# A retention and gated-MLP kernel on one core: w_sg transposed once, u's half of w_in in two loads, a new job order

## The chip, the cores and the metric

The kernel runs on one core of a Trainium2 chip, as one program. The metric is device microseconds of one execution, and the median over several runs is compared. Engines are named as in the profile: PE is TensorE, DVE is VectorE, ACT is ScalarE, POOL is GpSimd, SP is SyncE, which here only issues DMAs.

## The reference

Retention over 8 batches, 8 heads, 576 positions and head size 64, then a gated MLP that mixes along the sequence. All in float32.

```python
scores = scale * q @ k^T                       # per batch and head, 576 x 576
ret = scores * where(i >= j, gamma_h ** (i - j), 0)
x = (ret @ v), heads side by side              # 8 x 576 x 512
h = gelu_tanh(x @ w_in)                        # w_in 512 x 1024
u, v = h[..., :512], h[..., 512:]
v_n = (v - mean(v)) / sqrt(var(v) + 1e-6) * g_ln
v_s = einsum('ts,bsd->btd', w_sg, v_n) + b_sg  # w_sg 576 x 576, along the sequence
out = x + (u * v_s) @ w_out                    # w_out 512 x 512
```

## The kernel before

Two batches make a pair of 1152 rows, nine tiles of 128. Tile 4 (MID) holds the last 64 rows of the first batch and the first 64 of the second. A pair is worked in five blocks (`RB`): blocks 0 and 1 of the first batch and 3 and 4 of the second have two tiles each, block 2 is the middle tile. There are four pairs, so 20 blocks and 36 tiles. Decay is put into q and v as row factors, so that inside a block a mask is enough, and what earlier positions of the batch give comes in through a running sum of k^T v.

For a block, SP loads q, k and v in float32 (`a_load`). POOL scales and casts them to bf16 (`a_prep`; for block 0, DVE does q and ACT does k). PE transposes q and k into PSUM (`a_T`) and DVE copies them to `qT`, `kT` (`a_Tev`); from block 10 on most of this is done by DMA transposes (`a_TX`). q of some blocks is loaded for two blocks at once (blocks 3 and 4, 5 and 6, and so on). Blocks 0, 1 and the middle ones are "joint": q and k share one tile and one transpose. Then PE makes scores (`a_S`), DVE masks them (`a_Sev`), PE makes k^T v (`a_Z`) and the retention output (`a_O`, `a_O2`), and ACT writes it as x, transposed, into `xT` (`a_Oev`).

For a tile, PE makes V's half of the hidden layer (`m_V`), ACT its gelu (`m_Vg`), DVE the statistics (`m_stats`), POOL the inverse root (`m_rs`), ACT the normalised `vn` (`m_norm`). PE makes u's half (`m_U`) and ACT its gelu (`m_Ug`). When a batch's tiles are normalised, PE multiplies by w_sg transposed (`m_W`, eight jobs a batch of five matmuls each), DVE multiplies the result into u (`m_Wg`), PE makes the output product (`m_O`), the residual is added (for the first pair by a PE matmul with the identity, for the others from an SBUF copy made by a DMA transpose, `m_X`), and SP stores it.

A batch's sequence begins at row 0 of a tile for the first batch of a pair and at row 64 of MID for the second, so w_sg transposed is kept twice: `wT[0]` for the first and `wT[1]`, shifted by 64 rows, for the second. w_sg is loaded by rows in float32 into a staging tile, cast by ACT into `wnat` (L413), and ten builds (`build_wT`, L921) of five PE transposes each, one for each 128 columns of each set, give ten PSUM tiles that DVE copies out (`evac_wT`, L925). `wnat` has 64 zero columns on either side, so that the shifted set falls out of the same transposes. Four spare rows of the middle tiles carry b_sg and the inverse of g_ln: `place_vmid` (L909, L910) and `place_wT` (L913, L914) write them from `row4b`, which comes from `to_col`, `col_math`, `to_rows` and `rows`.

The weights w_in (its halves `win_load(1)` for V, `win_load(0)` for u, 1 MB each), w_sg and w_out come through staging tiles that borrow the buffers of `xT` and `uT`. Each half of w_in is cast by DVE (L388) and ACT (L390) together, into the bf16 `w_in`.

Each of these steps is a job. A written-out list, `ORDER`, gives every job by its number; entries with f are filler matmuls of zeros (`fill`, L357). A planner (`Planner.follow`) takes each engine's jobs in the list's order, computes a start for each by estimated durations, and emits all jobs sorted by it. Every engine executes its own jobs strictly in that order, so a job that waits holds back all behind it on its engine. PSUM has two large buffers (tag `pp`: transposes, scores, retention outputs) and four small ones (tag `d`: everything else). SBUF buffers go round by tag: eight for loads of k, v and single q (`ld`), two for double q (`ldq`).

Before the first W job TensorE's queue holds, in this order of first appearance: filler, block 0's transposes and scores, filler, block 0's outputs, block 1, V of tiles 0 and 1, then block 2 and V of tiles 2 to 4 among the ten builds, block 3's transposes, u of blocks 0 to 2, scores and outputs of block 3. SP's queue begins: q, k, v of block 0, V's half of w_in, the last rows of w_sg, q, k, v of block 1, w_sg in two loads, q, k, v of block 2, q of blocks 3 and 4, u's half of w_in, k of 3, k of 4, v of 3, k of 6, v of 4, k of 5, q of blocks 5 and 6, w_out.

Of the kernel before, what the change touches and what calls it, by code (L numbers as in the profile page):

```python
# [17 lines left out]
SEM = {"PE": 205.0, "DVE": 35.0, "ACT": 35.0, "POOL": 35.0}  # L18
OVL = {"PE": 0.0, "DVE": 60.0, "ACT": 90.0, "POOL": 50.0, "SP": 0.0}
FETCH = (5400.0, 5000.0)  # L20
SWITCH = {("F", "Q"): 95.0, ("F", "T"): 95.0, ("Q", "F"): 140.0, ("Q", "T"): 90.0, ("T", "F"): 5.0, ("T", "Q"): 5.0}

# [58 lines left out]
class Planner:  # L81


    def __init__(self, bufs, free, slack=60.0, penalty=500.0, fill=None, fill_until=0.0):
        self.bufs, self.free = bufs, free
        self.slack, self.penalty = slack, penalty
        self.fill, self.fill_until = fill, fill_until
        self.jobs, self.order = [], {t: [] for t in bufs}
        self.dma_free, self.dmas, self.ring = 0.0, [], []
        self.mode, self.warm = None, False  # L90
        self.count, self.block, self.landed = 36, 1, 0.0
        self.port = 0.0
# [6 lines left out]
    def ready(self, j):  # L99
        t = max(self.free[j.eng], j.since)  # L100
        if j.port:
            t = max(t, self.free["POOL"])
        if j.eng == "POOL":
            t = max(t, self.port)
        if j.behind is not None:
            if j.behind.start is None:
                return None
            t = max(t, j.behind.start + 100.0)
        for d in j.deps:
            if d.start is None:  # L110
                return None
            lat = 166.0 if (d.eng == "DVE" and j.eng == "POOL") else SEM.get(d.eng, 0.0)
            if d.eng == j.eng:
                lat = j.lag if j.eng == "PE" else 60.0
            if j.eng == "PE" and d.eng != "PE":
                lat += 20.0
            t = max(t, d.out + lat)
        took = {}
        for b in j.new:
            o, n = self.order[b.tag], self.bufs[b.tag]  # L120
            at = len(o) - n + took.get(b.tag, 0)
# [10 lines left out]
    def place(self, j, t):  # L132
# [31 lines left out]
        if j.port:  # L164
            self.port = j.out
# [1040 lines left out]
```

## Time and profile before

| | |
|---|---|
| median of 3 runs | 213.02 us (211.63 to 214.35) |
| span of the profiled execution, first to last instruction | 211.8 us |
| mean granted TensorE clock | 0.992 |
| busy: PE, DVE, ACT, POOL | 193.5, 146.7, 116.3, 117.9 us |
| moved by DMA | 50.45 MB, mean 238 GB/s |

The profiled execution has no time apart from its span; the three timed runs stand on both sides of it. "Busy" counts time in which at least one instruction of the engine runs. A row of a timeline gives start, duration, engine, line, operation, output and input, and in brackets how long the engine stood idle before it and what ended that. A row of windows gives the stretch and its length, each engine's busy time with the count of instructions, the granted clock, the DMA share and GB/s. A group's row gives busy time and mean nanoseconds after the first bar, idle time and releasers after the second.

### The profile page before, as it was taken

The page shows a single profiled execution, that of the slowest core. Times are in us where ns is not written, and L with a number is a line of the kernel's source. Part 1 is how long each engine was busy: PE and PEld are TensorE (multiplying, and loading weights), DVE is VectorE, ACT ScalarE, POOL GpSimd, SP SyncE. Part 2 cuts the span into 40 slices and gives each one's busy share as a digit, 9 for nine tenths or more (in the row PEclk, how much of TensorE's full clock was granted, in tenths as well). Part 3 has the DMA queues.
Part 4 walks back from the last instruction along what each step waited for, and adds up shares of the span by engine and source line. Part 5 has one row for each costly group of instructions (what it writes and reads, how often), then busy time and mean ns, then how long its engine had stood idle before and what let it go on. Part 6 is the DMA issues. An engine that isn't in the chain of part 4 may idle for free.

```text
span 211.8 us, 7654 instructions
## 1 busy us (share of the span) xinstructions
PE 193.5 (91%) x3257; PEld 134.4 (63%) x3288; DVE 146.7 (69%) x287; ACT 116.3 (55%) x207; POOL 117.9 (56%) x169
## 2 busy tenths in 40 slices
PE   7995598799999999989999979989989999999992
PEld 6873366576677666757676657656647676565660
DVE  4585487978767688648767647778676757977483
ACT  5233656993696753784775745617544574363400
POOL 8738375897599699920849598044349440322000
PEclk9999889999999999999999999999999999999999
DMA  5999899999799999999898989999789986936685
GB/s 157 334 274 323 140 377 273 259 347 320 146 316 319 317 208 289 181 258 326 245 253 110 219 155 345 237 129 248 197 217 264 254 193 187 225 115 149 176 249 198
DMA packets 94228, 50.45 MB, mean 238 GB/s; under 512 B 45354, under 2 KB 87602, under 8 KB 94194
## 3 DMA queue, kind: packets, MB, share of 16 engines
q1 hardware_dynamic: 94176, 49.97, 96.9%
q8 instruction: 25, 0.41, 0.9%
q14 instruction: 9, 0.07, 0.2%
q10 hardware_dynamic: 18, 0.00, 0.0%
HBM read 32.79 MB, written 9.44 MB: 199 GB/s over the span
## 4 chain that ended last, share of the span: by engine, by line
PE 62%; DMA 16%; SPq 5%; POOL 5%; DVE 3%; ACT 3%; issue 3%; POOLq 0%; ACTq 0%
PE wp L807 15%; PE op L838 11%; PE hu L788 11%; PE hv L741 11%; PE pp L673 5%; DMA xT<-in_moe_w_sg_dram 4%; DMA xT<-in_moe_w_in_dram 4%; PE pp L591 3%; DMA ld<-in_k_dram 3%; DMA kT<-kb 3%; SPq L560 3%; DMA ld<-in_q_dram 2%; PE zp L627 2%; SPq L457 2%; POOL vb L503 2%
## 5 line engine op out<-in xcount | busy, mean ns | idle before, releaser
L604 DVE TENSOR_TENSOR ret<-pp,msk 128x1024 bf16<-128x1024 f32 x32 | 38.7, 1216 | 6.4 <-PE pp L591 6.4
L503 POOL TENSOR_TENSOR vb<-ld,gpow 128x1024 bf16<-128x1024 f32 (+1 forms) x20 | 34.6, 1731 | 14.7 <-DMA ld<-in_v_dram 9.1
L807 PE MATMUL wp<-wT,vn 128*128 128x288 bf16 x256 | 40.8, 286 | 0.0
L788 PE MATMUL hu<-xT,w_in 128*128 128x256 bf16 (+1 forms) x320 | 36.7, 262 | 0.2 <-ACT zb L659 0.2
L741 PE MATMUL hv<-w_in,xT 128*128 128x512 bf16 x125 | 35.1, 380 | 1.4 <-issue 0.3
L817 DVE TENSOR_TENSOR uT<-wp,uT 128x288 bf16<-128x288 f32 x64 | 27.9, 449 | 11.5 <-PE wp L807 11.0
L838 PE MATMUL op<-w_out,uT 128*128 128x512 bf16 (+1 forms) x136 | 34.3, 373 | 0.6
L730 ACT ACTIVATE xT<-pp 128x512 bf16<-128x512 f32 (+1 forms) x40 | 20.6, 552 | 25.8 <-PE pp L673 24.0
L788 PEld LDWEIGHTS <-w_in 128*128 128x128 bf16 x320 | 28.2, 98 | 7.0 <-issue 0.5
L756 DVE BATCH_NORM_STATS2 bst<-vg 128x6 f32<-128x512 f32 x36 | 24.7, 687 | 10.1 <-ACT vg L748 10.0
L776 ACT ACTIVATE vn<-vg,mv 128x512 bf16<-128x512 f32 x32 | 25.3, 807 | 11.1 <-POOL mv L764 11.0
L748 ACT ACTIVATE vg<-hv 128x512 f32<-128x512 f32 x36 | 21.3, 594 | 17.0 <-PE hv L741 13.3
L807 PEld LDWEIGHTS <-vn 128*128 128x128 bf16 x256 | 24.2, 98 | 8.4 <-issue 0.2
L761 POOL TENSOR_SCALAR mv<-mv 128x2 f32<-128x2 f32 (+1 forms) x20 | 4.5, 224 | 42.2 <-DVE mv L757 38.3
L503 POOL TENSOR_TENSOR qb<-ldq,gpow 128x1024 bf16<-128x1024 f32 x14 | 26.5, 1902 | 0.9 <-DMA ldq<-in_q_dram 0.8
L798 ACT ACTIVATE uT<-hu 128x512 bf16<-128x512 f32 x36 | 20.9, 595 | 7.9 <-PE hu L788 7.9
L855 DVE TENSOR_TENSOR ob<-op,xr 128x512 f32<-128x512 f32 (+1 forms) x28 | 18.4, 668 | 6.1 <-PE op L838 5.8
L838 PEld LDWEIGHTS <-uT 128*128 128x128 bf16 x148 | 13.7, 98 | 11.5
L741 PEld LDWEIGHTS <-xT 128*128 128x128 bf16 x144 | 13.2, 98 | 11.6 <-ACT xT L730 0.2
L807 PE MATMUL wp<-wT,vmid 128*128 128x288 bf16 x64 | 18.3, 287 | 0.0
L493 POOL CAST kb<-ld 128x1024 bf16<-128x1024 f32 x14 | 14.4, 1038 | 4.3 <-DMA ld<-in_k_dram 4.2
L762 POOL TENSOR_TENSOR mv<-mv,mhalf 128x2 f32<-128x2 f32 (+1 forms) x20 | 13.7, 686 | 1.7
(100 smaller groups left out, 248.9 us busy)
## 6 DMA issues: line engine op xcount, KB each, us to landing
out_dram<-ob SPq DMA_DIRECT2D x35, 256.0 KB, 3.5
ld<-in_k_dram SPq DMA_DIRECT2D x16, 512.0 KB, 6.9
ld<-in_v_dram SPq DMA_DIRECT2D x16, 512.0 KB, 6.7
ldq<-in_q_dram SPq DMA_DIRECT2D x7, 1024.0 KB, 8.4
xT<-in_moe_w_sg_dram SPq DMA_DIRECT2D x2, 576.0 KB, 9.0
ld<-in_q_dram SPq DMA_DIRECT2D x2, 512.0 KB, 6.3
xT<-in_moe_w_in_dram SPq DMA_DIRECT2D x1, 1024.0 KB
ld<-in_q_dram SPq DMA_DIRECT2D x8, 128.0 KB, 5.9
```

The costliest lines, as they stand in the source:

```text
L503: ve.tensor_tensor(dst, src, g.unsqueeze(len(src.shape) - 1).to_broadcast(list(src.shape)), op=Alu.mult)
L604: ins = nc.vector.tensor_tensor(ret[:].rearrange("p r (k t) -> p (r k) t", k=2), sc[:].rearrange("p r (k t) -> p (r k) t", k=2), (msk2 if ...
L730: nc.scalar.activation(dst, src, Act.Copy)
L741: ins = nc.tensor.matmul(hv[:], xTs[p][:, m, kk, :], w_in[:, kk, F2:], start=(kk == 0), stop=(kk == KK - 1))
L748: unfence(nc.scalar.activation(vgs[i][:], cur.pop(("hv", i))[:], Act.Gelu_apprx_tanh), ("V", i))
L756: nc.vector.bn_stats(bst[:], vgs[i][:])
L776: nc.scalar.activation(vn[:], vg[:], Act.Identity, scale=mv[:, s, 2:3], bias=mv[:, s, 3:4])
L788: ins = nc.tensor.matmul(hu[:, n, :], w_in[:, kk, 128 * c:128 * c + 128], xTs[p][:, m:m + w, kk, :], start=(kk == 0), stop=(kk == KK - 1), ...
L798: unfence(nc.scalar.activation(uTs[p][:, c0:c1, 128 * m:128 * m + 128 * w], cur.pop(("hu", i, half))[:], Act.Gelu_apprx_tanh), ("U", i, half))
L807: ins = nc.tensor.matmul(ps[:], vns[t0 + j][e][:, 128 * c:128 * c + 128], wT[e][j][:, half * HS:(half + 1) * HS], start=(j == 0), stop=(j ...
L817: ins = nc.vector.tensor_tensor(uTs[p][:, c, col:col + HS], cur.pop(("wp", b, c, half))[:], uTs[p][:, c, col:col + HS], op=Alu.mult)
L838: ins = nc.tensor.matmul(op[:], uTs[p][:, c, r], w_out[:, c, cs], start=(p >= XP and c == 0), stop=(c == KK - 1), skip_group_check=True)
```

## The change

`wT[0]` and `wT[1]` become one tile each. Five builds, one for each 128 rows of w_sg, transpose into PSUM, and DVE copies each into `wT[0]`; the last holds 64 rows. ACT copies `wT[0]` into `wT[1]` shifted by 64 partitions, in nine copies of 64 x 576 (`shift_wT`). The jobs of batch 0 wait for the five copies and one `place_wT`; those of batch 1 for the nine shifts and the other. The memset of `wT[0]`'s spare rows goes.

u's half of w_in comes in two loads of half the columns, each cast by DVE and ACT. u's first job for a two-tile block waits for the first half, the second job for the second. For block 0 the transposes leave PSUM in two halves, by DVE and ACT.

The planner's estimates are gone: the new `ORDER` is emitted as it stands. Its only fillers are `f1` and the new order is different for every engine. TensorE now begins: one small filler, `to_col`, block 0's transposes, both `to_rows`, block 0's scores and k^T v, block 1's transposes, k^T v of block 1, block 0's outputs, block 1's scores, V of tile 0, and so on; transposes of block 3's q stand ahead of block 2's; u's first job stands after V of tile 2, and four jobs of u for blocks 3 and 4, after k^T v of block 4, stand before the first W job (two of them) and among the first W jobs (two). SP's queue begins: k, q, v of block 0, q, v, k of block 1, V's half of w_in, q of blocks 3 and 4, q and k of block 2, the last rows of w_sg, the first half of u's w_in, v of 2, k of 3, k of 4, the second half of u's w_in, w_sg's first load, v of 3, w_sg's second, v of 4, k of 5, k of 6, q of blocks 5 and 6, w_out. `place_vmid` moves on ACT from behind V's gelu of tile 4 to before that of tile 0. On DVE `col_math` and the two `rows` stand before block 0's mask, and the cast of V's half of w_in before block 1's `a_Tev`.

```diff
     def plan(self):
-        if ORDER:
-            return self.follow(ORDER)
...
+        self.done = [self.fill(int(x[1:])) if x[0] == "f" else self.jobs[int(x)] for x in ORDER.split()]
...
-    wnat = consts.tile([128, SB, S + 128], BF, name="wnat")
+    wnat = consts.tile([128, SB, S + 64], BF, name="wnat")
...
-    wT = [[consts.tile([128, S], BF, name=f"wT{e}_{j}") for j in range(SB)] for e in range(2)]
+    wT = [consts.tile([128, SB, S], BF, name=f"wT{e}") for e in range(2)]
...
+        parts = 1 if half else 2
+        w = F2 // parts
...
+        def g(part, a, eng):
+            src = wst["in", half][:, 2 * a:2 * a + 2, w * part:w * part + w]
...
+    def a_Tev(b, t, c=None):
...
+        if c is None:
+            ins = nc.vector.tensor_copy(dst, src)
+        elif c == 0:
+            ins = nc.vector.tensor_copy(dst[:, 0], src[:, 0])
+        else:
+            ins = nc.scalar.activation(dst[:, 1], src[:, 1], Act.Copy)
...
-    def build_wT(e, j):
-        c0 = (64 if e == 0 else 0) + 128 * j
-        tp = psD.tile([128, SB * 128], BF, name="wtp", tag="d")
...
-    def evac_wT(e, j):
-        r = slice(0, NB0) if (e, j) == (0, SB - 1) else slice(NB0, 128) if (e, j) == (1, 0) else slice(0, 128)
-        nc.vector.tensor_copy(wT[e][j][r, :], cur.pop(("wtp", e, j))[r, :S])
+    def build_wT(t):
+        tp = psD.tile([128, SB, 128], BF, name="wtp", tag="d")
+        cur["wtp", t] = tp
+        for j in range(SB):
+            nc.tensor.transpose(tp[:, j, :], wnat[:, t, 128 * j:128 * j + 128], ident[:])
+
+    def evac_wT(t):
+        w = min(128, S - 128 * t)
+        nc.vector.tensor_copy(wT[0][:, :, 128 * t:128 * t + w], cur.pop(("wtp", t))[:, :, :w])
+
+    def shift_wT(j, up):
+        if up:
+            nc.scalar.activation(wT[1][NB0:, j, :], wT[0][:NB0, j, :], Act.Copy)
+        else:
+            nc.scalar.activation(wT[1][:NB0, j, :], wT[0][NB0:, j - 1, :], Act.Copy)
...
-                     deps=xd + [jw[0, 0], jw[0, 1]] + ([] if fst else [J["U", p]]), ins=34 // w,
+                     deps=xd + (ju[2 * half:2 * half + 2] if w == 2 else ju) + ([] if fst else [J["U", p]]), ins=32 // w,
...
-                             deps=[J["n", i] for i in tls] + [jt[e, j] for j in range(SB)] + [j_pw, j_pv] + ([] if fst else [J["W", 2 * p, 0, 0]]),
+                             deps=[J["n", i] for i in tls] + jt[e] + [j_pv] + ([] if fst else [J["W", 2 * p, 0, 0]]),
```

More of the change, by code (lines that the diff above doesn't have):

```diff
@@ L81, with __init__ @@
 class Planner:
[L84 to L92, printed above, removed]
+    def __init__(self, bufs, fill):
+        self.bufs, self.fill, self.jobs = bufs, fill, []
     def add(self, *a, **k):
@@ L97, in add @@
         return j
[L99 to L121, printed above, removed]
-            took[b.tag] = took.get(b.tag, 0) + 1
-            if at >= 0:
-                for u in o[at].users:
-                    if u.start is None:
-                        return None
-                    t = max(t, u.out + (SEM.get(u.eng, 0.0) if u.eng != j.eng else 0.0))
-        if j.nbytes and len(self.dmas) >= 8:
-            t = max(t, self.dmas[-8])
-        return t + SWITCH.get((self.mode, j.mode), 0.0)
@@ L132, in place @@
-    def place(self, j, t):
-        j.start = t
-        if j.nbytes:
-            n = j.nbytes / j.run / 16.0 / j.parts
-            at = t
-            for part in range(j.parts):
-                if part and len(self.dmas) >= 8:
-                    at = max(at, self.dmas[-8])
-                room, full = 160.0 - n, 0.0
-                for end, m in reversed(self.ring):
-                    room -= m
-                    if room < 0:
-                        full = end
-                        break
-                self.dma_free = max(self.dma_free, at + 1500.0) + 120.0 + (14.0 + 0.0285 * j.run) * n
-                at = max(at + j.dur / j.parts, full)
-                self.ring.append((self.dma_free, n))
-                j.out = self.dma_free + 1500.0
-                self.dmas.append(j.out)
-            self.free[j.eng] = at
-        else:
-            late = 0.0
-            if j.eng == "PE":
-                while self.count + j.ins > 256 * self.block:
-                    at = t + j.dur * (256 * self.block - self.count) / j.ins + late
-                    late += max(0.0, self.landed - at)
-                    self.landed = max(self.landed, at)
-                    self.landed += FETCH[self.landed > 32000.0]
-                    self.block += 1
-                self.count += j.ins
-            j.out = t + j.dur + late
-            self.free[j.eng] = j.out - OVL[j.eng]
-        if j.port:
-            self.port = j.out
-        if j.mode is not None:
-            self.mode = j.mode
-        for b in j.new:
-            self.order[b.tag].append(b)
@@ L171, in follow @@
-    def follow(self, order):
-        line = {e: [] for e in self.free}
-        for x in order.split():
-            j = self.fill(int(x[1:]), 0.0 if x[0] == "f" and self.warm else 2700.0) if x[0] == "f" else self.jobs[int(x)]
-            self.warm = self.warm or x[0] == "f"
-            line[j.eng].append(j)
-        done = []
-        while any(line.values()):
-            heads = [(t, l[0]) for l in line.values() if l for t in [self.ready(l[0])] if t is not None]
-            t, j = min(heads, key=lambda x: x[0])
-            self.place(j, t)
-            line[j.eng].pop(0)
-            done.append(j)
-        self.done = sorted(done, key=lambda j: j.start)
-        return max(j.out for j in done)
@@ L229, in emit @@
+    def plan(self):
+        self.done = [self.fill(int(x[1:])) if x[0] == "f" else self.jobs[int(x)] for x in ORDER.split()]
     def emit(self):
+        seen = set()
         for j in self.done:
+            assert all(d in seen for d in j.deps)
+            seen.add(j)
             j.fn()
+        assert all(j in seen for j in self.jobs)
 @with_exitstack
@@ L350, with fill @@
     nc.gpsimd.memset(mhalf[:], -0.5)
-    def fill(n, cold):
+    def fill(n):
         bf = Buf("d")
@@ L357, in f @@
                 nc.tensor.matmul(scr[:, :w], warm[:, :128], warm[:, :w], start=True, stop=True, skip_group_check=True)
-        return Job("PE", 216.0 * n + cold, 0.0, f, new=bf, mode="F", ins=2 * ((n + 1) // 2))
-    pl = Planner(BUFS, dict(PE=1200.0, DVE=3100.0, ACT=5100.0, POOL=4550.0, SP=800.0), slack=PR["slack"], penalty=PR["pen"],
-                 fill=fill, fill_until=45000.0)
+        return Job("PE", 216.0 * n, 0.0, f, new=bf, mode="F", ins=2 * ((n + 1) // 2), what=n)
+    pl = Planner(BUFS, fill)
     add = pl.add
@@ L390, in g @@
                 nc.scalar.activation(dst, src, Act.Copy)
[L391 to L394 removed]
+        ld = []
+        for part in range(parts):
+            ld.append(add("SP", 600.0, -1e6, lambda part=part: f(part), deps=ld[-1:], new=None if part else bf, uses=[bf] if part else [],
+                          nbytes=(1 << 20) // parts, run=4 * w, what=("win", half)))
+        for part in range(parts):
+            for a, eng, dur in ((0, "DVE", 65.0 + 625.0 / parts), (1, "ACT", 185.0 + 875.0 / parts)):
+                j = add(eng, dur, 0.0, lambda part=part, a=a, eng=eng: g(part, a, eng), deps=[ld[part]], uses=[bf],
+                        what=("winc", half, a), port=eng == "DVE")
+                jw[half, part, a] = j
+                out.append(j)
         stage[half] = bf
[L396 removed]
+        return out
     def sg_load():
```

140 lines of the change are left out of this document (47 added, 93 removed), and 66 rows, old and new, of the table ORDER.

## The prediction

> **What bounds the kernel now.** I read the page first, then busy time and granted clock by stage, then each engine's timeline up to 54 us.
>
> ```profile
> span 211.8 us, 7654 instructions
> PE 193.5 (91%) x3257; PEld 134.4 (63%) x3288; DVE 146.7 (69%) x287; ACT 116.3 (55%) x207; POOL 117.9 (56%) x169
> PE   7995598799999999989999979989989999999992
> PE 62%; DMA 16%; SPq 5%; POOL 5%; DVE 3%; ACT 3%; issue 3%; POOLq 0%; ACTq 0%
> ```
>
> TensorE is busy 91% of the span and holds 62% of the chain that ended last. From the tenth slice on its row is nearly all nines; what is missing lies in the first nine slices, 48 us. TensorE's work sets the time from there on, and the opening sets how early that work can run densely. The windows say how much is open there:
>
> ```profile
> 8.00:16.00 8.00, 7.85 (x160) 6.46 (x158) 6.20 (x15) 1.90 (x3) 3.50 (x2) 1.00 1.15 308
> 16.00:26.00 10.00, 5.14 (x124) 3.31 (x123) 5.26 (x8) 5.14 (x10) 5.98 (x7) 0.95 0.98 231
> 26.00:36.00 10.00, 9.16 (x193) 6.14 (x193) 7.82 (x18) 5.29 (x11) 6.18 (x7) 0.88 1.04 319
> 36.00:46.00 10.00, 8.30 (x218) 6.80 (x217) 7.81 (x13) 9.68 (x17) 8.37 (x13) 1.00 1.03 293
> 54.00:92.00 38.00, 36.59 (x763) 25.82 (x764) 28.36 (x50) 26.09 (x51) 32.55 (x38) 1.00 1.06 255
> 92.00:184.00 92.00, 88.16 (x1442) 59.90 (x1454) 63.63 (x121) 52.86 (x96) 46.05 (x63) 1.00 1.03 226
> ```
>
> After the length stand PE, PEld, DVE, ACT and POOL busy, then granted clock, DMA share, GB/s. From 8 to 46 us TensorE idles 0.15 + 4.86 + 0.84 + 1.70 = 7.6 us. Part of its busy time there is filler on a tile of zeros (the same first window, that tile alone):
>
> ```profile
> 8.00:16.00 8.00, 5.78 (x27) 4.47 (x25) 1.00 1.15 308
> ```
>
> So 7.6 + 5.8 = 13.4 us of TensorE's time between 8 and 46 us hold no useful work, while DMA moves 231 to 319 GB/s: the opening waits for data.
>
> **The change part by part.** *w_sg transposed once by row tiles.* Ten builds of five transposes become five. Summed over the transposes' tile from 8 to 46 us (PE and DVE busy):
>
> ```profile
> sum 38.00, PE 4.65 DVE 4.39; mean PE 1.16 DVE 1.10
> L925 DVE COPY wT<-wtp 128x576 bf16<-128x576 bf16 x8 | 3.5, 450 | 3.4 <-PE wtp L921 3.3
> ```
>
> TensorE is spared half of 4.65, 2.3 us; at the full clock nearer 5 x 0.4 = 2.0. I take 2.0, since some of the fifty ran at a lower clock (rows under the fillers). VectorE copies four times 640 columns instead of 576 and once 320: by 450 ns, about 4 x 0.49 + 0.27 = 2.2, and is spared 2.2 us. It is not the bound anywhere in the windows, so this counts nothing.
>
> *The shifted set, by ScalarE.* Nine copies of 64 x 576. The nearest rows are copies of that width on ScalarE:
>
> ```profile
> L413 ACT ACTIVATE wnat<-ld 64x576 bf16<-64x576 f32 x1 | 0.7, 668 | 0.0
> L914 ACT ACTIVATE wT<-row4b 4x576 bf16<-4x576 bf16 x1 | 0.7, 682 | 0.0
> 48.00:64.00 16.00, 10.29 (x20) 1.00 0.99 259
> 36.00:48.00 12.00, 11.65 (x21) 1.00 1.04 307
> ```
>
> 9 x 0.68 = 6.1 us more for ScalarE (the two windows are ScalarE alone). In the new queue the nine stand between the evacuations of blocks 3 to 7: all of what they take is queued ahead of x for blocks 4 to 7 and of the gelu that frees TensorE's PSUM buffers. From 36 to 48 us ScalarE has 0.35 us left, from 48 to 64 us 5.7 us. The four vmid placements move out of this stretch, ahead of the first gelu:
>
> ```profile
> 39.27 0.63 ACT L909 ACTIVATE vmid<-row4b 4x512 bf16<-4x512 bf16 x1
> 41.18 0.63 ACT L910 ACTIVATE vmid<-row4b 4x512 bf16<-4x512 bf16 x1
> ```
>
> That returns 4 x 0.63 = 2.5. So 11.65 + 10.29 + 6.1 - 2.5 = 25.5 of 28 us: it fits with 2.5 to spare. I take 0; the bounds are 0 (covered by those 2.5 us) and 3.6 us (if ScalarE's 6.1 us of idle time there stays as waits, 25.5 + 6.1 - 28).
>
> *u's half of w_in in two loads.* One more issue on SP and one more pair of casts.
>
> ```profile
> 24.62 0.58 SPq L381 DMA_DIRECT2D uT<-in_moe_w_in_dram  x1
> 34.60 1.06 ACT L390 ACTIVATE w_in<-uT 128x1024 bf16<-128x1024 f32 x1 [0.80 <-DMA uT<-in_moe_w_in_dram]
> 35.98 1.93 PE L788 MATMUL hu<-xT,w_in 128*128 128x256 bf16 x24 [0.20 <-ACT zb L659]
> ```
>
> SP pays 0.58 us ahead of block 4's v and what follows. Now u's first matmuls wait until 35.98 for one load of 1 MB that landed near 34.6. The first half stands in the new queue behind eleven loads instead of fourteen, with 6.4 MB up to and with it; at the 0.26 MB/us of the opening (v's load of block 3, the last of 10 MB, is used at 40.70) that is about 26 us, and the second half about 33. TensorE then has u's matmuls of blocks 0 and 1 to fill gaps near 26. That is where the idle time is used.
>
> *First block's transposes leave PSUM in halves.* VectorE and ScalarE copy side by side:
>
> ```profile
> 8.89 1.22 DVE L555 COPY qT<-pp 128x2048 bf16<-128x2048 bf16 x1 [2.48 <-PE pp L540]
> 10.03 0.16 DVE L870 COPY col<-tp 128x9 f32<-128x9 f32 x1
> 11.92 0.18 DVE L880 TENSOR_TENSOR col<-colr,col 128x10 bf16<-128x10 f32 x1
> 12.94 2.35 DVE L604 TENSOR_TENSOR ret<-pp,msk 128x1024 bf16<-128x1024 f32 x2
> 14.40 1.90 POOL L503 TENSOR_TENSOR qb<-ld,gpow 128x1024 bf16<-128x1024 f32 x1 [3.63 <-DMA ld<-in_q_dram]
> 18.16 0.81 PE L741 MATMUL hv<-w_in,xT 128*128 128x512 bf16 x3 [0.16 <-ACT xT L730]
> ```
>
> The copy falls from 1.22 to about 0.7 us beside it. But the column arithmetic (10.03 to 12.1) now stands ahead of it on VectorE, and the row transposes ahead of the scores on TensorE, so the two masked scores still end near 15.3, as now; I take 0. V's half of w_in moves behind six loads of 0.52 MB, so it lands when 4.2 MB are in (near 18 instead of 12.1; block 1's v, 4.3 MB in, comes at 19.19 now). Queued behind its casts on VectorE is block 1's transposed copy, on ScalarE block 0's x; the first hv starts about 1.5 us later than 18.16. In exchange block 1's q is prepared at 10.5 instead of 14.40. These cancel before the anchor below.
>
> *The fillers go.* All but one small one. What they may cover is the clock:
>
> ```profile
> 20.00:24.00 4.00, 1.36 (x35) 0.64 (x35) 3.30 (x5) 1.46 (x3) 1.09 (x1) 1.00 1.00 146
> 24.00:28.00 4.00, 2.90 (x66) 2.47 (x66) 1.61 (x4) 2.14 (x5) 2.70 (x3) 0.62 0.85 238
> 25.11 1.25 PE L921 MATMUL wtp<-ident,wnat 128*128 128x128 bf16 x10 [2.55 <-ACT wnat L413]
> 31.01 0.73 PE L921 MATMUL wtp<-ident,wnat 128*128 128x128 bf16 x10
> ```
>
> After a stretch with 1.36 of 4 us busy the clock falls to 0.62, and ten transposes take 1.25 instead of 0.73 us. Useful work before 26 us is about 7.85 + 5.14 - 5.78 = 7.2 us; if all ran 1.7 times as long that is 5 us, within the 13.4 us free. I take 0 to 0.5, in the last term. [...]
>
> *The new order, and the sum.* I anchor it where DMA must feed TensorE. The loads up to and with block 5's q are the same set in both queues (12.6 MB), so it should land when it does now:
>
> ```profile
> 48.49 3.76 POOL L503 TENSOR_TENSOR qb<-ldq,gpow 128x1024 bf16<-128x1024 f32 x2 [0.48 <-DMA ldq<-in_q_dram]
> 53.69 0.64 PE L540 MATMUL pp<-ident,qb 64*128 64x64 bf16 x32
> 61.12 0.87 PE hu L788 x8
> ```
>
> GpSimd is done at 52.25; the transposes can start at 52.3 instead of 53.69: 1.4 us. In the new TensorE order four jobs of u for blocks 3 and 4 (4 x 0.87 = 3.5 us) stand ahead of them that stood behind; the five W jobs, V to tile 6 and output products to block 4 are ahead in both. The five spared builds lie ahead as well, so their 2.0 us are part of how this fits and are not added: 1.4 + 3.5 = 4.9 us gained. The new work fits: 3.5 + 1.4 against 13.4 + 2.0 free.
>
> What can take it back is GpSimd, busy 32.55 of 38 us from 54 to 92: to run 4.9 us earlier it must use nearly all its 5.4 idle. Bounds 0 to 2; I take 0.5, with the clock. So -4.9 + 0.5 = -4.4: a span of 207.4. Runs of 211.63, 213.02 and 214.35 stand around the span of 211.8; the median is 1.2 above. Forecast **208.6 us**, 2.1% under.
>
> **The rivals.** *A, the opening's gain is swallowed.* u's jobs ahead don't fit because of the cold clock or VectorE waiting in order for w_in; 1.4 us remains of the anchor: 211.6. For it: the same 12.6 MB, the 0.62. Against: 13.4 us of room. [...]
>
> *B, the opening is used better than by the anchor.* If two thirds of 13.4 are filled, because 256-byte loads are spread (DMA is at 146 GB/s from 20 to 24) and GpSimd keeps up: 213.0 - 9 = 204. For it: 13.4 us of room, four of them with DMA far under its rate. Against: the same bytes must land first, and GpSimd has 5.4 us.
>
> *C, ScalarE becomes the bound.* Place: its queue from the first shift to the last, some 40 to 65 us. Price: the nine copies, 6.1, less 2.3 spared on TensorE: 213.0 + 3.8 = 216.8; with the 3.6 bound and the 2.0, 214.6. It decides once ScalarE has no idle left in that stretch and TensorE waits on x or on PSUM. For it: 11.65 of 12 busy. Against: 5.7 idle behind it and the vmid placements gone.
>
> *D, the change doesn't do what it says.* The moved waits make fewer jobs early: this ends at A's 211.6.
>
> **How the numbers follow.** Forecast 0.50 (206.3 to 210.5, 0.3 of it under the 2% line at 208.76, 0.2 above); A with D 0.20; B 0.18; C 0.12, half of it over 217.3. Two per cent is about what a measurement of this kernel can tell from no change. Faster 0.30 + 0.18 = 0.48; within 0.20 + 0.20 + 0.06 = 0.46; slower 0.06. The range takes in A, most of B and C's lower bound: 203.5 to 214.6.
>
> **What would show it.** Right: TensorE transposes block 5's q near 52.3 with u's jobs of blocks 3 and 4 before it; the wT transposes sum to about 2.3 us; the shifts take 0.68 us each and no PE wait over 1 us points to ScalarE from 40 to 66 us; idle past 54 us stays under 7 us. Wrong: block 5's q prepared well before 52 or after 54, granted clock low through 26 us with u's jobs late, GpSimd or ScalarE named before TensorE's idle time in 54 to 92.

## The result, and the profile after

Beside the kernel before the changed kernel took 212.27 us (median of 20 runs, 209.62 to 214.66) against 213.49 (20 runs): ratio 0.9918 [0.9889, 0.9948]. Two later comparisons gave 1.0045 [1.0005, 1.0086] (212.89 against 212.60) and 1.0020 [0.9977, 1.0064] (213.03 against 212.73). The ratios use fast runs alone, which are those within 1.5% of the fastest run of the same kernel, so they hang on that one run; the medians of all runs give 0.994, 1.001 and 1.001. The first interval overlaps neither of the other two, so the change is worth something between 0.8% less time and 0.5% more: no gain that can be relied on, where 2.1% were forecast.

The page of the changed kernel (span, TensorE's row of slices, chain):

```profile
span 209.0 us, 7540 instructions
PE   1226687998999979999998999999999999999992
PE 81%; DVE 7%; DMA 5%; issue 3%; ACT 2%; POOL 0%; SPq 0%; DVEq 0%; POOLq 0%; ACTq 0%
```

TensorE holds more of the chain than before, but its first three slices, 16 us, hold 1 to 2 tenths and the next four hold 6 to 8 tenths, and VectorE, which had 3%, now has 7%. The windows (columns as before) say the same in numbers:

```profile
8.00:16.00 8.00, 2.13 (x26) 1.28 (x26) 7.60 (x14) 0.90 (x1) 6.60 (x4) 1.00 1.13 320
16.00:26.00 10.00, 6.61 (x202) 5.08 (x203) 8.00 (x11) 5.77 (x11) 5.66 (x4) 1.00 1.21 262
```

From 8 to 16 us VectorE is busy 7.60 of 8 us with 14 instructions (15 instructions took 6.20 before), and TensorE does 2.13 us of work. Timelines of that stretch, of VectorE, of GpSimd and, last, of ScalarE:

```profile
8.86 0.18 DVE L757 RECIPROCAL colr<-colr 128x4 f32<-128x4 f32 x1
8.96 1.79 DVE L758 COPY colr<-col 128x5 f32<-128x5 f32 x1
10.66 0.16 DVE L761 CAST col<-colr 128x8 bf16<-128x8 f32 x1
10.85 1.75 DVE L762 TENSOR_TENSOR col<-colr,col 128x8 bf16<-128x8 f32 x1
12.72 1.76 DVE L762 TENSOR_TENSOR col<-colr,col 128x10 bf16<-128x10 f32 x1
14.39 0.68 DVE L435 COPY qT<-pp 128x1024 bf16<-128x1024 bf16 x1
8.82 1.90 POOL L377 TENSOR_TENSOR vb<-ld,gpow 128x1024 bf16<-128x1024 f32 x1 [1.25 <-DMA ld<-in_v_dram]
10.68 1.90 POOL L377 TENSOR_TENSOR qb<-ld,gpow 128x1024 bf16<-128x1024 f32 x1
12.54 1.90 POOL L377 TENSOR_TENSOR vb<-ld,gpow 128x1024 bf16<-128x1024 f32 x1
15.10 1.02 ACT L437 ACTIVATE qT<-pp 128x1024 bf16<-128x1024 bf16 x1 [8.73 <-DVE qT L435]
```

This is the core of the case. Three instructions of the column arithmetic, on 5 to 10 columns, take 1.75 to 1.79 us each; the same lines take 0.14 to 0.18 where GpSimd rests. Each ends within 0.04 us of the end of the GpSimd instruction beside it (10.75 and 10.72, 12.60 and 12.58, 14.48 and 14.44). The column arithmetic runs from 8.07 to 14.48, 6.4 us instead of 2.1, and queued behind it on VectorE are block 0's transposed copy, on TensorE the row transposes and block 0's scores. ScalarE's half of that copy (last row) starts only when VectorE's half has ended, so the two halves take 0.68 and 1.02 us one behind the other. TensorE's rows, the first of the kernel before, the others of the changed one:

```profile
11.07 0.42 PE L591 MATMUL pp<-qT 64*64 64x128 bf16 x16
16.17 0.64 PE L473 MATMUL pp<-qT 64*64 64x128 bf16 x15 [0.71 <-ACT qT L437]
24.98 1.89 PE L623 MATMUL hv<-w_in,xT 128*128 128x512 bf16 x4
27.57 1.04 PE L623 MATMUL hv<-w_in,xT 128*128 128x512 bf16 x4
32.61 0.83 PE L670 MATMUL hu<-xT,w_in 128*128 128x256 bf16 x6 [0.99 <-ACT w_in L258]
56.29 0.64 PE L414 MATMUL pp<-ident,qb 64*128 64x64 bf16 x32
```

Block 0's scores start at 15.15 (one matmul) and 16.17 (the next fifteen) instead of 11.07, the first hv at 24.98 instead of 18.16, block 5's q at 56.29 instead of 53.69.

### The profile page after: what moved, and what is told of

The parts are those of the page before. It is cut to its first block, busy times and chain, and to the rows that moved or that the text cites. A ratio compares the mean times of both kernels' runs of the same rounds, so it can differ in the third digit from the quotient of the medians.

```text
span 209.0 us, 7540 instructions
## 1 busy us (share of the span) xinstructions
PE 184.2 (88%) x3213; PEld 124.6 (60%) x3213; DVE 149.9 (72%) x282; ACT 122.3 (59%) x218; POOL 117.4 (56%) x168
## 4 chain that ended last, share of the span: by engine, by line
PE 81%; DVE 7%; DMA 5%; issue 3%; ACT 2%; POOL 0%; SPq 0%; DVEq 0%; POOLq 0%; ACTq 0%
PE wp L689 18%; PE hv L623 15%; PE op L720 15%; PE hu L670 14%; PE pp L555 7%; PE pp L473 5%; PE zp L509 3%; DMA ld<-in_q_dram 3%; PE pp L414 3%; DMA kT<-kb 2%; DVE col L762 2%; PE op L715 1%; DVE colr L758 1%; PE wtp L799 1%; DVE bst L638 1%
## 5 line engine op out<-in xcount | busy, mean ns | idle before, releaser
L623 PE MATMUL hv<-w_in,xT 128*128 128x512 bf16 x144 | 36.9, 387 | 0.0
L720 PE MATMUL op<-w_out,uT 128*128 128x512 bf16 (+1 forms) x148 | 35.8, 373 | 0.0
L689 PEld LDWEIGHTS <-vn 128*128 128x128 bf16 x256 | 24.4, 98 | 9.9 <-issue 1.2
L689 PE MATMUL wp<-wT,vmid 128*128 128x288 bf16 x64 | 17.8, 286 | 0.0
```

The lines of the kernel that those rows point to most:

```text
L623: ins = nc.tensor.matmul(hv[:], xTs[p][:, m, kk, :], w_in[:, kk, F2:], start=(kk == 0), stop=(kk == KK - 1))
L689: ins = nc.tensor.matmul(ps[:], vns[t0 + j][e][:, 128 * c:128 * c + 128], wT[e][:, j, half * HS:(half + 1) * HS], start=(j == 0), stop=(j ...
L720: ins = nc.tensor.matmul(op[:], uTs[p][:, c, r], w_out[:, c, cs], start=(p >= XP and c == 0), stop=(c == KK - 1), skip_group_check=True)
```

## The experiments

**Column arithmetic behind the masks (e1).** The changed kernel with four jobs moved:

```diff
 VectorE:  ... rows of block 0's q
-          column arithmetic, copy of block 0, mask, mask
+          copy of block 0, mask, mask, column arithmetic
 TensorE:
-          to_rows x2, scores of block 0, ... outputs of block 0
+          scores of block 0, ... outputs of block 0, to_rows x2
```

> The changed kernel with one thing moved: VectorE's column arithmetic stands behind block 0's two masks instead of ahead of block 0's copy out of PSUM, and the two row transposes and row copies follow it. Theory 1 (the column arithmetic, standing beside GpSimd's preparation of v and q, is held up by GpSimd and pushes the opening back): block 0's scores start near 11 instead of 16.2 us, its masks end near 15, the column arithmetic shrinks from 6.4 us to under 4, the first hv starts near 20 to 21 instead of 24.98, and the time falls by 2 to 4 us. Rival 2 (the opening waits for w_in anyway): the first hv moves by under 1.5 us and the time by under 1. Rival 3 (the cold array sets it): scores start earlier, but the jobs stretch and the time moves by under 1.

It took 211.92 us, ratio 0.9946 [0.9897, 0.9996], span 207.8. The opening came as theory 1 has it, the time did not: 2 to 4 us were expected, and neither the median (212.27 for the changed kernel) nor the ratio (0.9918 there) shows more than 0.4 us. VectorE's timeline, and below it three rows of TensorE:

```profile
14.91 0.54 DVE L755 TENSOR_SCALAR colt<-col 128x4 f32<-128x4 f32 x1
15.98 0.14 DVE L759 COPY colr<-col 128x5 f32<-128x5 f32 x1
16.30 0.17 DVE L763 TENSOR_TENSOR col<-colr,col 128x8 bf16<-128x8 f32 x1
16.58 0.18 DVE L763 TENSOR_TENSOR col<-colr,col 128x10 bf16<-128x10 f32 x1
17.48 0.68 DVE L257 CAST w_in<-xT 128x1024 bf16<-128x1024 f32 x1
10.68 0.64 PE L474 MATMUL pp<-qT 64*64 64x128 bf16 x15 [0.75 <-ACT qT L438]
20.74 1.50 PE L624 MATMUL hv<-w_in,xT 128*128 128x512 bf16 x4
53.57 0.64 PE L415 MATMUL pp<-ident,qb 64*128 64x64 bf16 x32
```

The three slow rows are back at 0.14 to 0.18; one instruction that still meets GpSimd's cast (14.39 to 15.43) takes 0.54. The cast of w_in takes 0.68; in the changed kernel it met a GpSimd instruction and took 1.82. Block 0's scores start at 9.62 (one matmul) and 10.68 (fifteen), the first hv at 20.74. So the loss in the opening is shown to hang on where the column arithmetic stands; 2.1 of its 6.4 us are its own, 4.3 the lengthening beside GpSimd. But of 4.2 us at the first hv 2.7 are left at block 5's q (the last row) and 1.2 at the end of the span. Behind block 5's q TensorE's waits of 0.2 us and more sum to 3.7 us here and to 2.5 in the changed kernel, which is most of the 1.5 us lost there.

**The fillers put back (e2), and both (e3).**

```diff
-f1
+f24 at the start; f16 behind block 0's transposes; f5, f2 behind the row transposes; f5, f7 later
```

> The changed kernel with filler matmuls of zeros put back where TensorE idles in the first 24 us (before the first transposes, around the row transposes, after the first scores, ahead of block 1's scores), nothing else moved. Theory 1: block 0's scores still start near 16 us because VectorE is late, the first hv only gains its own doubled length (4 matmuls in 1.04 instead of 1.89 us) and the time moves by under 1 us. Rival 3: with the array warm, transposes take 0.64 instead of 1.04 us, hv starts 2 us earlier or more, and the time falls by 2 us or more. If fillers delay work behind them, it is slower by up to 1 us.

216.66 us, ratio 1.0151 [1.0076, 1.0226]: slower, by more than any of the expectations allowed. The fillers moved `to_col` and so the column arithmetic by 0.6 us, deeper into GpSimd's work, and now three of its instructions were caught whole, and a fourth in part (0.86 us):

```profile
8.87 1.82 DVE L755 TENSOR_SCALAR colt<-col 128x4 f32<-128x4 f32 x1
10.72 1.82 DVE L756 SCALAR_TENSOR_TENSOR colt<-col,colt 128x4 f32<-128x4 f32 x1
12.58 1.82 DVE L757 SCALAR_TENSOR_TENSOR colr<-colt,col 128x4 f32<-128x4 f32 x1
28.01 1.04 PE L624 MATMUL hv<-w_in,xT 128*128 128x512 bf16 x4
```

The column arithmetic ended at 15.96 instead of 14.48. The fillers behind it cost more: 2.50 and 1.22 us of them stand ahead of block 0's scores, which start at 20.45. The first hv took 1.04 us instead of 1.89, and came 3 us later. The waits of TensorE for nothing that the profile shows (taken up below) sum to 5.3 us past 40 us in this trace, against 2.8 in the changed kernel's, so the loss at the end has more than one part.

> Both of these together (column arithmetic behind the masks, fillers in the idle places), and block 1's copy out of PSUM ahead of the cast of w_in on VectorE. Theory 1 with rival 3 as a smaller part: block 1's scores start near 18 instead of 23.98 us, the first hv near 20, and the time falls by 3 to 5 us against the changed kernel. Rival 2: the first hv cannot start before about 20.5 since w_in lands at 18 to 20 us, and what is gained before is lost again by 56 us, where block 5's q is transposed: time falls by under 1.

211.33 us, ratio 0.9936 [0.9887, 0.9985], against 211.92 for the column arithmetic alone; 3 to 5 us below the changed kernel were expected. A third job moves with the two, block 1's copy out of PSUM, so the trial doesn't part the fillers from it. The first hv took 1.03 us at 22.98, yet block 5's q came at 54.34, later than the 53.57 without fillers. What the rival calls the cold array, the longer matmuls of the opening (first hv 1.50 us in e1, 1.03 here), is worth 0.6 us here or nothing.

**The w_sg part alone (e4).** The kernel before, with its order and fillers, but five builds in the first five places of the ten and nine shifts on ScalarE from 48 us on.

> One part of the change alone: the kernel before, with its own order and fillers, but w_sg transposed once by row tiles (five builds in the first five of the ten places) and the shifted set copied by ScalarE in nine copies from 48 us on. By the sum of the prediction this is worth 2.0 us of TensorE, if ScalarE's nine copies cost nothing: time 1 to 2 us under the kernel before. Rival (ScalarE's 6.1 us are on the path): no change or 1 to 3 us over it. Rival (the spared builds stood in idle time of the opening anyway): no change.

212.93 us, ratio 0.9998 [0.9949, 1.0047], where 1 to 2 us less were expected. The 2 us of TensorE time spared don't show, nor do the shifts. That the builds lay in idle stretches is argued: a gain and a cost of one size would look the same. For it speaks that no wait of TensorE from 44 to 64 us, where the shifts run, names ScalarE.

**u's half in one load (e10).** The changed kernel with `parts = 1` for u's half, at the first half's place.

> The changed kernel with u's half of w_in in one load of 1 MB at the place of the first half and two casts, everything else in the changed order. My theory of the two loads (they bring TensorE's first u jobs forward): u's half lands whole at about 31 to 33 us instead of its first half near 28, the wait of the first u jobs for the cast of w_in grows from 1.0 to between 3 and 5 us, block 5's q is transposed 1 to 3 us later than 56.3, and the time is 0.5 to 2.5 us longer. Rival (a load that is hidden anyway): under 0.5 us.

213.51 us, ratio 0.9986 [0.9946, 1.0027], between the changed kernel's 0.9918 and 1.0045, which lie too far apart to show 0.5 us. The trace speaks for the rival: VectorE casts the whole load at 28.27 (the first half of two: 28.36), so 1 MB is there by then, and the first u jobs wait 1.42 us, not 3 to 5. What they wait for is ScalarE, which comes to its cast at 32.37, after x and V's gelu:

```profile
28.27 0.69 DVE L257 CAST w_in<-uT 128x1024 bf16<-128x1024 f32 x1
32.37 1.05 ACT L259 ACTIVATE w_in<-uT 128x1024 bf16<-128x1024 f32 x1
33.47 0.83 PE L671 MATMUL hu<-xT,w_in 128*128 128x256 bf16 x6 [1.42 <-ACT w_in L259]
```

**Waits for nothing that the profile shows.** In the changed kernel TensorE still stands idle after 48 us, three times for "issue". Its rows, and windows from 0 to just before each of these three, in which the figures of interest are the counts of matmuls and weight loads:

```profile
50.33 0.30 PE L555 MATMUL pp<-ret,vb 64*64 64x128 bf16 x6 [0.61 <-issue]
75.73 0.44 PE L509 MATMUL zp<-vb,kb 64*64 64x64 bf16 x29 [1.26 <-issue]
114.14 0.30 PE L689 MATMUL wp<-wT,vn 128*128 128x288 bf16 x1 [0.92 <-issue]
0.00:50.32 50.32, 32.13 (x731) 22.23 (x732) 36.12 (x70) 30.50 (x52) 32.97 (x57) 1.00 1.03 281
0.00:75.72 75.72, 56.18 (x1243) 39.15 (x1243) 56.34 (x107) 52.69 (x92) 52.70 (x79) 1.00 1.05 283
0.00:114.13 114.13, 93.68 (x2010) 64.83 (x2010) 82.91 (x156) 80.12 (x144) 81.26 (x114) 1.00 1.04 261
```

1243 - 731 = 512 and 2010 - 1243 = 767: the waits stand 4 and 6 times 128 pairs of weight load and matmul apart, that is whole multiples of 256 instructions. The trace also has packets of 16 KB on a queue of kind "instruction"; one landed at 48.86, one at 74.28, one at 112.78, each 1.36 to 1.47 us before TensorE went on; the three took 1.04 to 1.18 us and had started 3.2 to 4.5 us after the place 128 weight loads before. So I formed a theory: TensorE's instructions come in blocks of 256, and where a block is worked off before the next is there, TensorE waits. The next trials put instructions ahead to test it.

> The changed kernel with 82 matmuls of 16 columns (164 instructions of TensorE) put at the very start, where TensorE waits from 1 to 5 us for its first data. Nothing else is moved. Theory of the instruction blocks: every wait without a releaser so far stands at an instruction whose number leaves 193 when divided by 256, 1.35 to 1.6 us after a 16 KB packet of TensorE's instruction queue has landed; 164 more instructions move these places, and by the trace of the changed kernel the shortest stretches between two of them fall from 4.3 and 4.7 us to 3.9, 4.0, 4.0 and 4.2 us. So its waits without a releaser leave 2497 and 4033 for new places, again 193 over a multiple of 256, their sum grows from 2.8 us to between 3.5 and 6, and the time is 0.5 to 3 us longer than the changed kernel's. Rival (these waits belong to the matmuls at which they stand, for a reason that the profile lacks): they stay at the same matmuls, now 164 records later, and the time is the same within 0.5 us.

> The column arithmetic behind the second mask, and 38 matmuls of 16 columns (76 instructions) at the very start. Theory of the instruction blocks: by the trace of the first such run the shortest stretches between two places of the row 193 over a multiple of 256 become 4.5, 5.0, 5.1 and 5.5 us instead of 4.7, 4.8, 5.0 and 5.2, so the waits without a releaser move to other matmuls and their sum falls from 3.1 us to between 1 and 2.5; the span is 206 to 207.3. Rival: the waits stay at the same matmuls, the span is 207.8 as without the 38.

235.68 us, ratio 1.1132 [1.1065, 1.1199], and 224.56, 1.0537 [1.0439, 1.0636]. Neither tests the theory. In f32 each of these matmuls stands twice in the trace (166 weight loads for 83 matmuls of the program, `f1` among them, whose one matmul is x2 in the changed kernel's trace too), so not 164 and 76 instructions were put ahead but 328 and 152; and at 0.21 us from one record to the next, in spite of 16 columns, they hold TensorE from 1.24 to 36.84 us in the first and to 18.05 in the second. They show one thing: in the first, block 0's scores start 24.4 us later than in the changed kernel (39.56 against 15.15), and the end comes 22.8 us later. What lies behind absorbs little of so late an opening. Beside them ran

> The changed kernel itself, run beside the next three. Both theories: span near 209.0 us, ratio to the kernel before 0.992 as measured; TensorE's waits without a releaser again at the same instructions, the 1474th, 2498th and 4034th of its records (0.61, 1.26 and 0.92 us).

> The column arithmetic behind the second mask again, now side by side with the changed kernel. If the 2.7 us that it was ahead at block 5's q are worth 1.2 at the end, its span is 207.8 and its time 1.2 us below the changed kernel's in this call; if the first look at it was luck, the two come out within 0.5 us of each other.

with 212.89 us, 1.0045 [1.0005, 1.0086], and 212.23, 0.9953 [0.9906, 1.0001]. The profiled spans were 209.8 and 207.6; block 5's q stood at 56.98 and 53.73. So the move is worth 0.7 us by the medians. TensorE's waits stood at the same three matmuls in the first (51.02, 75.90 and 114.89 us). The next matmuls were made of 64 rows and 16 columns in bf16:

```diff
-            for w in [256] * (n // 2) + [128] * (n % 2):
+            for _ in range(n - 1000):
+                nc.tensor.matmul(scr[:16, :16], warmb[:], warmb[:], ...)
```

> The changed kernel with 60 matmuls of 16 columns, 64 rows, bf16 (120 instructions of TensorE) at the very start, in the idle time from 1.2 to 5.2 us; the ones of 128 rows and f32 in the earlier trial took 0.375 us each, 23 us for 82, and so delayed the opening instead of shifting instructions. Theory of the instruction blocks: the waits without a releaser leave the places 1474, 2498 and 4034 for matmuls 120 records earlier in the work, the shortest stretches between two block ends become 3.9, 4.0, 4.1 and 4.7 us where the changed kernel has 4.3, 4.7, 5.0 and 5.2, and with a new block ready some 5.6 us after the end of the last one but one (a delay of about 3 us, 1.2 for the packet, 1.45 behind it) the sum of such waits past 40 us grows from 2.0 to 2.8 us to 4 to 6: 1 to 3 us slower than the changed kernel. Rival (the waits belong to the matmuls where they stand): same matmuls, same time within 0.5 us of 212.3 to 212.9.

> The column arithmetic behind the second mask and 38 such short matmuls (76 instructions) at the very start. Theory of the instruction blocks: other matmuls wait, and the sum of the waits without a releaser past 40 us is 1 to 2.5 us (3.1 and about 2.9 in the two traces without the 38); span 206.0 to 207.5, median 0 to 1 us below the kernel with the column arithmetic moved alone (211.9 and 212.2). Rival: no change, waits at the same matmuls.

The f32 ones had taken 0.43 us each, 35.6 us for 83, not 0.375 and 23. Of the new ones 60 ended by 3.6 us, within idle time, and block 0's scores start at 15.04 and 16.06, as in the changed kernel. Still the time is 215.97, ratio 1.0117 [1.0061, 1.0174], where the changed kernel had 212.3 to 213.0 and ratios of 0.9918 to 1.0045: 1.5 to 4 us more. TensorE's waits and the counts up to them, first of e8 (an execution of 218.04 us):

```profile
48.71 0.26 PE L514 MATMUL zp<-vb,kb 64*64 64x64 bf16 x2 [3.45 <-issue]
103.09 0.29 PE L419 MATMUL pp<-ident,qb 64*128 64x64 bf16 x4 [1.88 <-issue]
0.00:48.70 48.70, 30.07 (x728) 21.61 (x732) 33.81 (x69) 27.56 (x47) 31.15 (x57) 1.00 1.02 282
0.00:103.08 103.08, 82.01 (x1742) 57.49 (x1755) 72.03 (x136) 68.41 (x121) 70.10 (x102) 0.98 0.96 252
```

Then of e9 (211.10 us, ratio 0.9900 [0.9859, 0.9941]):

```profile
111.65 0.34 PE L514 MATMUL zp<-vb,kb 64*64 64x64 bf16 x17 [1.45 <-issue]
0.00:111.64 111.64, 92.50 (x1995) 65.06 (x2010) 76.63 (x152) 78.08 (x139) 80.29 (x112) 0.98 1.03 266
```

And of the kernel before:

```profile
90.63 0.30 PE L673 MATMUL pp<-qT,zb 64*64 64x128 bf16 x5 [0.94 <-issue]
0.00:90.62 90.62, 80.19 (x1614) 58.88 (x1627) 64.53 (x133) 55.02 (x98) 68.17 (x98) 0.98 1.04 269
```

The weight loads (second count; some matmuls lack a record) are 732, 1755, 2010 and 1627: divided by 128 they leave 92, 91, 90 and 91, as the changed kernel's 732, 1243 and 2010 do (92, 91, 90). The matmuls that wait are others each time, the place in the stream is the same. That is the theory's forecast, against the rival's (the same matmuls, the same time); such waits past 40 us sum to 5.5 us in e8, where 4 to 6 were expected. Behind each of its two long waits the granted clock reads 0.5 (48.7 to 51.8 us and 103.0 to 106.4), and sixteen matmuls of hu at 48.91, just behind the first, take 3.29 us where sixteen at 57.81 take 1.91, so a wait costs more than its own length. In e9, as forecast, the waits at zp near 74 were gone and came elsewhere (0.74 and 1.45). The other traces say the same: all 37 waits of TensorE over 0.5 us for "issue" past 40 us, in 17 traces, stand at the same place of 128 weight loads, give or take one, and end 1.25 to 1.66 us after such a packet has landed. The place of the block ends is shown to matter; 76 instructions gained nothing sure (211.10 here, 211.92 and 212.23 without them, not side by side).

**q of blocks 3 and 4 in two loads (e11).** With the column arithmetic moved, GpSimd waited 6.64 us for q of blocks 3 and 4 (its row names a ScalarE copy that had just ended; the last piece of the load landed at 21.91) and TensorE 2.07 us for GpSimd.

```diff
-            nc.sync.dma_start(f_[:], src[2 * p + e, :, ...])
+            for h0, h1 in ((0, H // 2), (H // 2, H)) if b == 3 and sup else ((0, H),):
+                nc.sync.dma_start(f_[:, h0:h1], src[2 * p + e, h0:h1, ...])
```

> The column arithmetic behind the second mask, and the 1 MB load of q of blocks 3 and 4 in two loads of 512 KB, four heads each. If the landings are what bounds the opening once the column arithmetic is out of the way (GpSimd waited 6.64 and 6.80 us for this load, to 22.07 and 22.09, and TensorE 2.07 and 1.18 us for what GpSimd makes of it), GpSimd's first piece starts at 20.3 to 21.0 us, TensorE's wait there falls under 1 us, and block 5's q is transposed about 1 us earlier than 53.6; at the end 0.3 to 1 us. If the landings don't bound it (GpSimd's own 5.8 us of work do, or u's first half at 27 us), block 5's q stays within 0.3 us of 53.6 and the time the same.

210.75 us, ratio 0.9893 [0.9840, 0.9946]. GpSimd's timeline, and TensorE's wait:

```profile
19.79 1.90 POOL L379 TENSOR_TENSOR qb<-ldq,gpow 128x1024 bf16<-128x1024 f32 x1 [4.23 <-DMA ldq<-in_q_dram]
23.03 1.04 POOL L379 TENSOR_TENSOR qb<-ld,gpow 128x512 bf16<-128x512 f32 x1 [1.34 <-DMA ld<-in_q_dram]
25.99 1.07 PE L416 MATMUL pp<-ident,qb 64*128 64x64 bf16 x48 [1.04 <-POOL qb L379]
53.14 0.64 PE L416 MATMUL pp<-ident,qb 64*128 64x64 bf16 x32
```

GpSimd starts 2.3 us earlier, then waits for block 2's q; TensorE's wait halves, block 5's q comes 0.4 us earlier, which lies between the two expectations (1 us, and within 0.3). So a landing bounds GpSimd at this point, and little of it reaches block 5's q. What the split load alone is worth at the end was not measured side by side.

**Side by side (a2, e11 again, e12).**

> The changed kernel a third time, beside the two next. Expected between the two earlier comparisons: 0.992 to 1.0045 of the kernel before, span 209 to 211, block 5's q transposed at 56 to 57.5 us.

> Column arithmetic moved and q of blocks 3 and 4 in two loads, again, beside the changed kernel. If the lead of 3.1 us at block 5's q (53.14 against 56.3) reaches the end, its median is 2 to 3 us below the changed kernel's in this call; if waits behind it take most of it back, 0.3 to 1.2 us.

> The same with the 38 short matmuls at the start, which move the block ends by 76 instructions. Theory of the instruction blocks: sum of the waits without a releaser past 40 us 1 to 2.2 us (2.2 in both of the two traces that it is made from), at other matmuls, median 0 to 1 us below the one without them. Rival: no difference, under 0.3 us either way.

213.03 us (1.0020), 210.43 us (0.9892 [0.9832, 0.9951]) and 210.30 us (0.9874 [0.9821, 0.9926]). Block 5's q stood at 57.62 in the first and 53.34 in the second: of 4.3 us there 3.5 are left in the spans (211.6 and 208.1) and 2.6 in the medians, as the first of the two expectations has it. The 38 short matmuls changed nothing in the time, as e12's rival said, though the waits moved to other matmuls (77.62 and 111.24 us) and summed to 2.1 us, as the theory said. With or without them, this version beats both kernels by a little over 1%.

## Why the prediction was right or wrong

*Builds, right in size.* The transposes now take

```profile
L799 PE MATMUL wtp<-ident,wnat 128*128 128x128 bf16 x25 | 2.1, 220 | 0.0
L808 ACT ACTIVATE wT<-wT 64x576 bf16<-64x576 bf16 x5 | 3.3, 678 | 0.1
36.00:64.00 28.00, 27.08 (x49) 1.00 1.03 278
```

2.1 us, about the 2.3 named as a sign. That they are "part of how this fits" and not a gain of their own fits e4's 0.9998.

*Shifts at price 0, right.* 0.68 us each (second row: five of the nine); ScalarE was busy 27.1 of 28 us from 36 to 64 (third row, ScalarE alone; 25.5 forecast), and still no wait of TensorE of 0.2 us or more points to it there. Rival C is out: a full engine off the path cost nothing that shows.

*u's two loads, wrong in what the jobs wait for.* The landing, "about 26 us", is not shown wrong: in the changed kernel the first half is there by 28.36, in e1 VectorE waited for it until 27.19, and e10's whole megabyte, 7.0 MB into the queue, by 28.27, which is about the rate assumed (0.25 MB/us). But the jobs that were to fill gaps near 26 waited for ScalarE, which casts in its own order, until 32.61, and one load does as well as two.

*First block and column arithmetic: the step that failed.* "The two masked scores still end near 15.3, as now; I take 0." They end at 20.3 (19.09 + 1.21). In e1, with the column arithmetic behind them, they end at 14.8 (13.59 + 1.22). The term is 5 us where I took 0. I costed the column arithmetic at its old duration in its new place: 2.1 us, and it took 6.4. The step even said that block 1's q would be prepared "at 10.5 instead of 14.40" (it was, at 10.68) and booked that as a gain; this preparation, with v of block 0 before it and v of block 1 behind, is what the column arithmetic ran into. A smaller part of the step is wrong too: the halves of the copy are not made "side by side". ScalarE's waits for VectorE's, in e1 as here, so that they take 1.7 us together instead of 0.7, where one copy took 1.22. The trace of before held the sign, one row of the column arithmetic beside GpSimd's only instruction of those microseconds:

```profile
8.87 1.90 POOL L503 TENSOR_TENSOR vb<-ld,gpow 128x1024 bf16<-128x1024 f32 x1 [1.33 <-DMA ld<-in_v_dram]
10.22 0.57 DVE L872 TENSOR_SCALAR colt<-col 128x4 f32<-128x4 f32 x1
10.83 0.16 DVE L873 SCALAR_TENSOR_TENSOR colt<-col,colt 128x4 f32<-128x4 f32 x1
```

An instruction on four columns took 0.57 us, ended at 10.79 as GpSimd's ended at 10.77, and the next one of the same width took 0.16. I read over it. What holds such an instruction up no row shows, only that it ends with GpSimd's and took 1.75 to 1.82 us instead of 0.14 to 0.18 where it was caught whole (the changed kernel and e2).

*"These cancel before the anchor", and the anchor: failed with it.* Block 5's q was prepared at 52.55, as forecast, since the bytes did land as now. But TensorE was behind: its transposes came at 56.29, 56.98 and 57.62 in three traces, not at 52.3. The first hv was 6.8 us later than before, not 1.5. Of the sum -4.9, the 1.4 became +2.6 to +3.9; the 3.5 for the four u jobs stood ahead as said. That makes -0.9 to +0.4, and the spans came out 2.8, 2.0 and 0.2 us below 211.8. What lies between, 1.9, 1.8 and 0.6 us, is about what TensorE waited less behind block 5's q: its waits of 0.2 us and more sum to 4.5 us before and to 2.5, 2.7 and 3.8 in the three traces. So the whole miss in the span lies ahead of block 5's q. Moving the column arithmetic takes back 2.7 and 3.3 us of it (e1 and its repeat), and 0.7 us of the time; what holds the other 1.3 us and more is open beyond e11's 0.4. A further 0.5 us was a wrong offset: I put the median 1.2 us above the span, and the profiled executions whose time is known lie 1.7 above theirs (210.69 and 209.0).

*The fillers, 0 to 0.5: not contradicted.* Matmuls did take longer ahead of 27 us (four of hv 1.89 us at 24.98, then 1.04 at 27.57). But TensorE waited for others in that time, and e3, where the first hv takes 1.03, gains at most 0.6 us over e1. That A's time, 211.6, is near what came is luck: u's jobs did stand ahead, and what VectorE was late with was the column arithmetic, not a wait for w_in.

*GpSimd takes back 0.5: not seen.* Before, TensorE waited 1.8 us for GpSimd behind block 5's q; in the changed kernel's three traces it is 0.4 at most. What ends TensorE's waits there is mostly the instruction blocks, which I had at nothing: 2.2 us of the 2.5, where it was 1.2 before. Both effects stood in code that the change dropped: the old planner counts TensorE's instructions in blocks of 256 and adds a wait where a block is worked off early, and it keeps VectorE's casts of w_in out of GpSimd's time (`port`), though not the column arithmetic. The sign "prepared well before 52 or after 54" would have missed the failure: the preparation was on time, the engine behind it was not.

## What to carry to other kernels

When a transfer or a preparation moves earlier, list what will run beside it on the other engines, and look in the old trace for the same pair side by side: one row that is three times its sisters' length and ends with the neighbour's instruction is enough of a warning (0.57 us against 0.16 here). For a load, ask in which engine's queue its user stands, not only when it lands. Before dropping a planner, read what its estimates were there for. Time won or lost in an opening reached the end here by a fifth (0.7 of 3.3 us, e1 repeated) up to nearly whole (22.8 of 24.4), while work spared in an idle stretch showed no gain.

## What the runs showed of the hardware

VectorE's copies and products on 4 to 10 columns of SBUF took 1.75 to 1.82 us beside GpSimd's 128x1024 products, ten times their own 0.14 to 0.18. Not all are caught: copies out of PSUM weren't (0.68 beside a GpSimd cast), nor the reciprocal (0.18) or the statistics on SBUF (0.69 us, 16 times beside GpSimd and 20 times alone in the changed kernel). It goes the other way too: GpSimd's 128x512 product took 1.49 instead of 1.04 us while VectorE's w_in cast ran.

TensorE lost up to 3.45 us at a time (e8) at places that lie multiples of 128 weight loads, 256 instructions, apart, the block ends of the theory, going on 1.25 to 1.66 us after a 16 KB instruction packet had landed. Two of the three blocks behind which the changed kernel waits, with many matmuls on 64 rows, had been worked off in 4.7 and 4.9 us. 120 instructions in idle time ahead cost 1.5 to 4 us by moving these places (e8).

The granted clock read 1.00 in windows in which matmuls took nearly twice their later time (1.89 us at 24.98, 1.04 at 27.57). The changed kernel's trace has no record of the clock ahead of 27.02 us, and the first hv of 1.04 us comes at 27.57, so at the start the duration of a row is to be trusted, not that column.
